# Block-causal attention feeding a top-1 mixture of experts: GpSimd split of the first expert's weights, its subtraction, and a new order of steps for two batches

## The chip, the cores and the metric

One core of one Trainium2 chip runs the whole program as a single launch. The metric is device time in microseconds (us); the time before is the median of three runs. The engines are TensorE (PE; its weight loads are PEld), VectorE (DVE), ScalarE (ACT), GpSimd (POOL) and the queue of SyncE (SP), which issues most DMAs.

## What is computed

Attention over 8 batches, 8 heads, 576 positions and head size 64, masked by blocks of 64, in float32. Its output, 4608 tokens of 512 numbers, goes through a top-1 mixture of 8 experts:

```python
logits = x @ w_gate
e_idx = argmax(logits)                       # one expert per token
gate_w = exp(logits - max)[e_idx] / (sum(exp(logits - max)) + 1e-9)
eom = 1 / (1 + exp(-(x @ w_output_gate)))
for e in range(8):
    mask = e_idx == e
    ye = relu(x[mask] @ w1[e]) @ w2[e]       # w1 512x1024, w2 1024x512
    out[mask] = gate_w[mask] * eom[mask, e] * ye
```

## The kernel before

**Attention.** The program walks 32 pairs of heads (p = 0 to 31, four to a batch b). Pair p's scores and softmax, pair p-1's transposes and pair p-2's products with V are interleaved by a table, `PLAN` (line 299). Its names are: S0 to S4, the scores of the five query tiles on PE; M0 to M4, their row maxima and the scaled biases on DVE (lines 396, 400, 404); E0 to E4, the exponentials on ACT (line 411; A and B are the two heads); F0 to F6, the transposes of the probabilities on PE (lines 445, 458); C0 to C6, the copies of these out of PSUM on ACT (line 1084); V0, V1 and VM, the products with V on PE (lines 480, 488); X and XM, the copies of these on ACT. Two PSUM buffers hold scores, so S2 of a pair needs E4 of the pair before it to have read its buffer, and S1 of a pair needs E3. On PE, DVE and ACT the program order is the written order. On GpSimd and SP a scheduler sets it. Each engine works its own queue strictly in order.

**Turns.** Each "|" of PLAN is a turn, eight to a pair (0 to 7): every running generator of the list `later` advances to its next `yield`. In PLAN turn 0 and turn 1 come after C0, turn 2 after E0B, turn 3 after C4, turn 4 after M3, turn 5 after VM, turn 6 after M4 and turn 7 right behind it, before XM.

**A batch's end.** `finish_batch` (line 497) plays the 32 steps of `finish_steps` (line 505) for a batch whose four pairs are done; `pace` is how many steps go into a turn: 1 for batches 0 to 4 (four pairs long), 2 for batches 5 and 6 (two pairs long), 3 for batch 7. The steps: `logits` (PE, line 538) and `keep` (ACT, line 544), `turn_logits` and `turn_last` (PE), `scale_logits` and `scale_last` (DVE, lines 567, 579); `heads` (lines 587, 588) adds the heads' shares, on GpSimd for batches 0 to 4 and on DVE for 5 to 7; `choose` (DVE, lines 591 to 599) finds the maximum `mx` and the chosen expert `oh`, with `z` on GpSimd (line 600); `ranks`, `own` and `slots` find each token's place; `turn` and `store`, T(t) and K(t), write the five tiles of x out; `excess` (DVE, line 629) is `d = lg - mx`, `shares` (ACT, line 632) its exponential, `gather` three small sums on DVE (lines 635 to 637), `gate` an exponential on ACT (line 640), `weights` the token's weight on DVE (lines 643, 644), and `scatter` five indirect DMAs on GpSimd into the routing table (line 650).

**The first expert.** `load_first` (line 902) starts in pair 28. It picks the expert with most tokens of batches 0 to 5, fetches the ids (line 834) and rows (line 845) of its first tokens behind batch 5's scatter, and loads w1 and then w2 in four chunks of 128x1024. The chunks of w2 reuse the buffers of w1's. Each chunk is split into a high half (float16) and a low half (bfloat16): on GpSimd, `split` (line 872) does a chunk in four quarters of 128x256, each a cast (line 878) and a subtraction (line 879). The experts' matmuls (lines 1001 and 1030) begin after the attention; for all later experts the split is ACT's cast and DVE's subtraction (lines 874, 875).

Of the kernel before, what the change touches and what calls it, by code (L numbers as in the profile page):

```python
# [1 line left out]

# [7 lines left out]
BF16 = mybir.dt.bfloat16  # L10
# [4 lines left out]
ALU = mybir.AluOpType  # L15
# [11 lines left out]
def block_attention_top1_moe(  # L27
# [11 lines left out]
    nc = tc.nc  # L39
# [456 lines left out]

    def finish_batch(b, sums, xT, pace):

        for i, fns in enumerate(finish_steps(b, sums, xT)):
            for fn in fns:  # L500
                fn()
            if i % pace == pace - 1:
                yield

    def finish_steps(b, sums, xT):

        rec = small.tile([P, NT, H], F32, name="rec")
        lgT = sb.tile([P, S], F32, name="lgT", bufs=1)
# [10 lines left out]
        se = small.tile([P, NT], F32, name="se")  # L519
        sli = small.tile([P, NT], I32, name="sli")  # L520
        held = {}

        def bank():
            return ps_t.tile([P, 512], F32, name="ps_t")
# [18 lines left out]
        def keep(c0, c1):  # L543
            nc.scalar.copy(lgT[:, c0:c1], held[c0][:, 0:c1 - c0])  # L544

        def turn(t):
            r = ROWS[t]
            held["r", t] = pm = bank()
            for g in range(NP):
                nc.tensor.transpose(pm[0:r, P * g:P * g + P], xT[:, g, Q0[t]:Q0[t] + r], ident)  # L550

        def store(t):
            r = ROWS[t]
            xn = sb.tile([P, DM], F32, name="xn", bufs=4)
            nc.vector.tensor_tensor(
                xn[0:r].rearrange("p (h d) -> p h d", d=D), held["r", t][0:r].rearrange("p (h d) -> p h d", d=D),
                rec[0:r, t].unsqueeze(2).broadcast_to([r, H, D]), ALU.mult,
            )
            nc.sync.dma_start(x_d[b * S + Q0[t]:b * S + Q0[t] + r, :], xn[0:r])
# [22 lines left out]
            )  # L582

        def heads():
            eng = nc.gpsimd if b < B - 3 else nc.vector
            for w in (4, 2):
                eng.tensor_tensor(lh[:, :, 0:w], lh[:, :, 0:w], lh[:, :, w:2 * w], ALU.add)
            eng.tensor_tensor(L, lh[:, :, 0], lh[:, :, 1], ALU.add)

        def choose():  # L590
            nc.vector.tensor_reduce(mx, lg, AX.X, ALU.max)
            eq = small.tile([P, NT, E], F32, name="eq")
            nc.vector.tensor_tensor(eq, lg, mxb, ALU.is_equal)
            nc.vector.tensor_tensor(eq, eq, erev.unsqueeze(1).broadcast_to([P, NT, E]), ALU.mult)
            nc.vector.tensor_reduce(er, eq, AX.X, ALU.max)
            nc.vector.tensor_tensor(
                oh, er.unsqueeze(2).broadcast_to([P, NT, E]), erev.unsqueeze(1).broadcast_to([P, NT, E]), ALU.is_equal
            )
            nc.vector.memset(oh[64:128, LAST, :], 0.0)
            nc.gpsimd.tensor_tensor(z, lz, oh, ALU.mult)  # L600

        def ranks():
            held["p"] = pr = ps_a.tile([P, 512], F32, name="ps_a")
# [14 lines left out]
        def slots():  # L618
# [5 lines left out]
            sl = small.tile([P, NT], F32, name="sl")  # L624
            nc.vector.scalar_tensor_tensor(sl, er, -float(NTOK), rank, ALU.mult, ALU.add)
            nc.vector.tensor_scalar(sli, sl, float(E * NTOK), None, ALU.add)

        def excess():
            nc.vector.tensor_tensor(d, lg, mxb, ALU.subtract)

        def shares():
            nc.scalar.activation(d, d, AF.Exp)
# [13 lines left out]
        def scatter():  # L646
# [13 lines left out]

        big, end = (0, 512), (512, S)
        T, K = (lambda t: lambda: turn(t)), (lambda t: lambda: store(t))
        steps = [
            [lambda: logits(*end)], [lambda: keep(*end), lambda: logits(*big)], [lambda: keep(*big), recips], [turn_logits],
            [scale_logits], [turn_last], [scale_last], [heads],
            [], [], [T(0)], [K(0)], [], [choose], [], [],
            [], [T(1), ranks], [own, K(1), T(2)], [K(2)], [T(3), slots], [K(3)], [], [],
            [excess], [shares], [T(4)], [K(4)], [], [gather], [gate], [weights, scatter],
        ]
        return steps if b < B - 1 else [fns for fns in steps if fns]  # L670

# [198 lines left out]
                        tc.add_manual_dep(chained[0].ins, after.name, SYNC, reason="after the ids")  # L870

    def split(eng, hi, lo, src):
        if eng is nc.vector:
            nc.scalar.copy(hi, src)  # L874
            eng.tensor_tensor(lo, src, hi, ALU.subtract)  # L875
            return
        for at in quarters(src):
            eng.tensor_copy(hi[at], src[at])
            eng.tensor_tensor(lo[at], src[at], hi[at], ALU.subtract)

    def quarters(src):
        _, g, n = src.shape
# [19 lines left out]
    def load_first():  # L902

        route_first()
        fetch_ids(steps[0])
        fetch_ids(steps[1], (0, 1))
        fetch_x(steps[0])
        fetch_x(steps[1], (0, 1))
        with chain():
            ev = nc.sync.value_load(f_i[0:1, 0:1], min_val=0, max_val=E - 1)  # L910

        wc = {}

        def load(w, c):
            dt, nm = ((F16, "hh"), (BF16, "hl"))[c % 2]
            wc[c] = fs.tile([P, KF, 2, P], dt, name=nm).rearrange("p f h n -> p (f h n)").bitcast(F32)
            nc.sync.dma_start(quarter(w, wc[c]), rows_of(w, ev, c))

        for c in range(4):
            load(w1, c)  # L920
        for w, fn, r0, r1 in ((w1, split_w1, 13, 3), (w2, split_w2, 2, 2)):
            for r in range(r0):
                yield
            for c in range(4):
                fn(nc.gpsimd, 0, wc[c], c)
                if w is w1:
                    load(w2, c)
                for r in range(r1):
                    yield

    def buf(i):
        return 0 if i < 2 else (i - 1) % 2
# [337 lines left out]
```

## Time and profile before

| what | value |
|---|---|
| runs, us | 819.75 median (811.24, 819.75, 820.64) |
| the profiled execution | 814.11 us, of which the span is 812.4 us |
| PE busy | 734.6 us, 90% of the span |
| DVE, ACT, POOL busy | 546.8 (67%), 531.7 (65%), 339.4 us (42%) |
| attention and routing | about 0 to 440 us of the span; the experts from there to the end |

A row of a timeline is: start us, duration us, engine, line, operation, out<-in with shapes, how many instructions the row holds, and in brackets the idle time of that engine just before it and what ended it. L12 is line 12 of the kernel.

### The profile page before, as it was taken

What the parts mean: (1) busy time and instruction counts of PE and PEld (TensorE: products, weight loads), DVE (VectorE), ACT (ScalarE), POOL (GpSimd) and SP (SyncE); (2) the same over time, 40 slices, a digit from 0 to 9 for tenths busy, and PEclk for the clock granted to TensorE, in tenths of its full rate; (3) what the DMA queues carried; (4) which work ended last, traced back from release to release, by engine and by line L of the source; (5) the groups of instructions that cost most, each with busy time, mean ns of one, the idle gap of its engine ahead of it and who ended that gap; (6) DMA issues with size and microseconds to landing.
All of it is one profiled execution on the core that took longest, in us unless ns stands there. A gap on an engine that the chain in (4) does not pass through costs nothing. (4 is left out here: it accounts for less than half of the span.)

```text
span 812.4 us, 18753 instructions
## 1 busy us (share of the span) xinstructions
PE 734.6 (90%) x6918; PEld 516.4 (64%) x6918; DVE 546.8 (67%) x1060; ACT 531.7 (65%) x1189; POOL 339.4 (42%) x495
## 2 busy tenths in 40 slices
PE   5799999899999988843999999999999999999994
PEld 3577767666676656523676666956668566686652
DVE  6566867767676858588573786957679666795530
ACT  4799879788888876712511777855578655785530
POOL 5667755564747421494224732322422232410001
PEclk9899999999999999975999999999999999999998
DMA  8899988968884645641116799799999979731601
GB/s 157 163 187 198 222 180 149 226 139 185 148 204 90 138 83 134 162 128 28 47 60 231 186 274 297 230 282 332 315 303 364 297 156 332 239 73 40 234 28 42
DMA packets 256630, 147.88 MB, mean 182 GB/s; under 512 B 224144, under 2 KB 224208, under 8 KB 256528
## 3 DMA queue, kind: packets, MB, share of 16 engines
q1 hardware_dynamic: 248416, 127.30, 62.9%
q0 software_dynamic: 8112, 19.29, 7.6%
q8 instruction: 56, 0.92, 0.5%
q14 instruction: 46, 0.38, 0.2%
HBM read 126.03 MB, written 19.34 MB: 179 GB/s over the span
## 5 line engine op out<-in xcount | busy, mean ns | idle before, releaser
L1001 PEld LDWEIGHTS <-w1b 128*128 128x128 f16 (+1 forms) x2208 | 176.6, 98 | 25.3 <-issue 3.9
L411 ACT ACTIVATE pt<-ps_s,nbs 128x512 f32<-128x512 f32 (+4 forms) x282 | 155.2, 572 | 37.6 <-DVE nbs L404 35.9
L1001 PE MATMUL ps_s<-xt,w1b 128*128 128x256 f16 (+5 forms) x1920 | 175.5, 253 | 0.9 <-issue 0.4
L1030 PE MATMUL ps_t<-w2b,hh 128*128 128x512 f16 (+1 forms) x560 | 166.5, 379 | 0.0
L875 DVE TENSOR_TENSOR w2b<-w2f,w2b 128x1024 bf16<-128x1024 f32 x80 | 92.7, 1219 | 90.6 <-ACT w2b L874 77.7
L396 DVE TENSOR_REDUCE nmx<-ps_s 128x2 f32<-128x1024 f32 (+1 forms) x125 | 102.7, 821 | 64.2 <-PE ps_s L381 40.9
L1084 ACT COPY pT<-ps_t 128x512 f32<-128x512 f32 (+1 forms) x221 | 112.1, 555 | 36.2 <-PE ps_t L445 28.1
L1039 POOL DMA_INDIRECT out_dram<-ys,ids x38 | 51.8, 1363 | 161.0 <-ACT ys L1038 91.2
L445 PE MATMUL ps_t<-ident,pt 128*128 128x128 f32 x768 | 112.4, 283 | 5.5 <-ACT pT L1084 2.1
L1030 PE MATMUL ps_t<-w2b,hl 128*128 128x512 f16 x280 | 106.1, 379 | 0.0
L1038 ACT ACTIVATE ys<-ps_t,ids 128x512 f32<-128x512 f32 (+1 forms) x38 | 26.1, 686 | 111.8 <-PE ps_t L1030 95.5
L445 PEld LDWEIGHTS ps_t<-ident,pt 128*128 128x128 f32 x768 | 87.2, 144 | 15.8 <-ACT lgT L544 4.2
L1030 PEld LDWEIGHTS <-hh 128*128 128x128 f16 x560 | 54.3, 98 | 61.7 <-issue 0.7
L875 DVE TENSOR_TENSOR w1b<-w1f,w1b 128x1024 bf16<-128x1024 f32 x80 | 92.7, 1217 | 0.8 <-ACT w1b L874 0.7
L103 POOL TENSOR_TENSOR sp<-nat,sp 128x320 f16<-128x320 f32 x120 | 86.7, 742 | 3.9 <-DVE sp L102 2.5
L379 PE MATMUL ps_s<-tr,tr 128*128 128x512 f16 (+1 forms) x250 | 73.3, 309 | 12.6 <-ACT pt L411 12.5
L874 ACT CAST w1b<-w1f 128x1024 f16<-128x1024 f32 x80 | 78.4, 1045 | 2.8 <-DMA w1f<-in_moe_w_dram 2.4
L874 ACT CAST w2b<-w2f 128x1024 f16<-128x1024 f32 x80 | 77.7, 1043 | 0.4 <-DVE w2b L875 0.2
L480 PE MATMUL ps_a<-pT,va 128*64 128x384 f32 (+2 forms) x256 | 74.0, 412 | 0.0
L480 PE MATMUL ps_a<-pT,vb 128*64 128x384 f32 (+2 forms) x256 | 74.0, 412 | 0.0
L650 POOL DMA_INDIRECT tab_d<-idg,sli x40 | 38.9, 973 | 83.7 <-DVE idg L644 54.2
L380 PE MATMUL ps_s<-sw,tr 128*128 128x512 f16 (+1 forms) x250 | 71.3, 307 | 2.4 <-DVE sw L201 2.4
(220 smaller groups left out, 1206.5 us busy)
## 6 DMA issues: line engine op xcount, KB each, us to landing
w1f<-in_moe_w_dram SPq DMA_DIRECT2D x80, 512.0 KB
w2f<-in_moe_w_dram SPq DMA_DIRECT2D x80, 512.0 KB
nat<-in_k_dram SPq DMA_DIRECT2D x15, 576.0 KB
nat<-in_q_dram SPq DMA_DIRECT2D x15, 576.0 KB
x_d<-xn SPq DMA_DIRECT2D x32, 256.0 KB
va<-in_v_dram SPq DMA_DIRECT2D x32, 128.0 KB
vb<-in_v_dram SPq DMA_DIRECT2D x32, 128.0 KB
hh<-in_moe_w_dram SPq DMA_DIRECT2D x4, 512.0 KB
```

Source lines behind the costliest of these rows:

```text
L103: last_lo[0] = lo.tensor_tensor(sp[:, sl, 1, :], self.nats[i][:, sl], sp[:, sl, 0, :], ALU.subtract)
L379: nc.tensor.matmul(o, qq, k1[ab][:, 0:n], start=True, stop=False)
L380: nc.tensor.matmul(o, qq, k2[ab][:, 0:n], start=False, stop=False)
L396: nc.vector.tensor_reduce(nmx[t], at[t], AX.X, ALU.max, negate=True)
L411: last_exp[0] = nc.scalar.activation(probs[t][:, ab * n:(ab + 1) * n], at[t, ab], AF.Exp, bias=nbs[t][:, ab:ab + 1], scale=SCALE, accum_ou ...
L445: nc.tensor.transpose(held[i][:, P * j:P * j + P], probs[t][:, sl], ident)
L480: nc.tensor.matmul(pa[half, c0:512], vs[a][:, j, :], rows[:, a, j, c0 - P:512 - P], start=(j == 0), stop=(j == 3))
L874: nc.scalar.copy(hi, src)
L875: eng.tensor_tensor(lo, src, hi, ALU.subtract)
L1001: nc.tensor.matmul(ph[:, f4].rearrange("p (h n) -> p h n", n=w), wv[:, cc, f, :], xv[:, cc], start=(k == 0), stop=(k == 3 * KD - 1))
L1030: nc.tensor.matmul(py, hv[:, f, h], wv[:, f, :], start=(k == 0), stop=(k == 3 * KF - 1))
L1084: (nc.vector.tensor_copy if p >= B * NP and name in ("C1", "C3", "C5", "X") else nc.scalar.copy)(to, of)
```

## The change

The split of w1 moves to a generator of its own, `split_slowly`, that issues one quarter (cast and subtraction) per turn, sixteen in all. The split of w2 on GpSimd keeps only the subtractions; its casts, one of 128x1024 per chunk, go to ACT, a chunk per turn. `excess` is gone as a step: `d` is computed inside `choose`, on GpSimd for batches 0 to 5 and on DVE for 6 and 7; `z` and `heads` follow the same rule, so `heads` of batch 5 goes to GpSimd. Batches 5 and 6 get a list of steps of their own, one entry per turn. In the list of the others `shares` moves from turn 25 to 21, K(3) from 21 to 22, and `gather`, `gate`, `weights` and `scatter` each one turn earlier.

```diff
+        eng = nc.gpsimd if b < B - 2 else nc.vector
...
         def heads():
-            eng = nc.gpsimd if b < B - 3 else nc.vector
...
-            nc.gpsimd.tensor_tensor(z, lz, oh, ALU.mult)
+            eng.tensor_tensor(z, lz, oh, ALU.mult)
+            eng.tensor_tensor(d, lg, mxb, ALU.subtract)
...
+        lge, lgb, ke, kb = (partial(f, *c) for f in (logits, keep) for c in (end, big))
+        if pace == 2:
+            return [
+                [lge, lgb], [ke], [kb, recips], [turn_logits, turn_last], [scale_logits, T(0)], [scale_last, heads, K(0)], [], [choose],
+                [], [T(1), ranks], [own, K(1), T(2)], [K(2)], [slots, shares, T(3)], [gather, gate], [K(3), weights, scatter, T(4)], [K(4)],
+            ]
         steps = [
-            [lambda: logits(*end)], [lambda: keep(*end), lambda: logits(*big)], [lambda: keep(*big), recips], [turn_logits],
-            [scale_logits], [turn_last], [scale_last], [heads],
+            [lge], [ke, lgb], [kb, recips], [turn_logits], [scale_logits], [turn_last], [scale_last], [heads],
             [], [], [T(0)], [K(0)], [], [choose], [], [],
-            [], [T(1), ranks], [own, K(1), T(2)], [K(2)], [T(3), slots], [K(3)], [], [],
-            [excess], [shares], [T(4)], [K(4)], [], [gather], [gate], [weights, scatter],
+            [], [T(1), ranks], [own, K(1), T(2)], [K(2)], [T(3), slots], [shares], [K(3)], [],
+            [], [], [T(4)], [K(4)], [gather], [gate], [weights, scatter], [],
         ]
...
     def split(eng, hi, lo, src):
-        if eng is nc.vector:
-            nc.scalar.copy(hi, src)
-            eng.tensor_tensor(lo, src, hi, ALU.subtract)
-            return
+        nc.scalar.copy(hi, src)
+        for at in [(slice(None),) * 3] if eng is nc.vector else quarters(src):
+            eng.tensor_tensor(lo[at], src[at], hi[at], ALU.subtract)
+
+    def split_slowly(hi, lo, src):
         for at in quarters(src):
-            eng.tensor_copy(hi[at], src[at])
-            eng.tensor_tensor(lo[at], src[at], hi[at], ALU.subtract)
+            with tc.issue_after(last_exp[0].ins):
+                nc.gpsimd.tensor_copy(hi[at], src[at])
+                nc.gpsimd.tensor_tensor(lo[at], src[at], hi[at], ALU.subtract)
+            yield
...
+        for r in range(11):
+            yield
+        for c in range(4):
+            yield from split_slowly(w1b[0][:, 0, c], w1b[0][:, 1, c].bitcast(BF16), wc[c].rearrange("p (g m) -> p g m", g=KF))
+            load(w2, c)
+        for r in range(5):
+            yield
+        for c in range(4):
+            with tc.issue_after(last_exp[0].ins):
+                split_w2(nc.gpsimd, 0, wc[c], c)
+            yield
```

On DVE, in pair 30 (batch 6's end begins there), `heads` (line 587) stands ahead of M2 and M3 (`nmx_5723`, `nmx_5724`) before:

```order
L396 TENSOR_REDUCE nmx_5721<-ps_s 128x2
L404 TENSOR_SCALAR nbs_5726<-nmx_5721 128x1 x2
L567 TENSOR_TENSOR lh<-ps_t,rec 128x512
L579 TENSOR_TENSOR lh<-ps_t,rec 64x128
L587 TENSOR_TENSOR lh<-lh 128x5x64
L587 TENSOR_TENSOR lh<-lh 128x5x32
L588 TENSOR_TENSOR L<-lh 128x80
L396 TENSOR_REDUCE nmx_5723<-ps_s 128x2
L404 TENSOR_SCALAR nbs_5728<-nmx_5723 128x1 x2
L396 TENSOR_REDUCE nmx_5724<-ps_s 128x2
L404 TENSOR_SCALAR nbs_5729<-nmx_5724 128x1 x2
L555 TENSOR_TENSOR xn<-ps_t,rec 128x512
```

and after the change, on the same engine at the same place (`heads` is line 588, M2 and M3 are `nmx_5725` and `nmx_5726`, M4 is `nmx_5727`):

```order
L397 TENSOR_REDUCE nmx_5725<-ps_s 128x2
L405 TENSOR_SCALAR nbs_5730<-nmx_5725 128x1 x2
L397 TENSOR_REDUCE nmx_5726<-ps_s 128x2
L405 TENSOR_SCALAR nbs_5731<-nmx_5726 128x1 x2
L569 TENSOR_TENSOR lh<-ps_t,rec 128x512
L581 TENSOR_TENSOR lh<-ps_t,rec 64x128
L588 TENSOR_TENSOR lh<-lh 128x5x64
L588 TENSOR_TENSOR lh<-lh 128x5x32
L589 TENSOR_TENSOR L<-lh 128x80
L557 TENSOR_TENSOR xn<-ps_t,rec 128x512
L401 TENSOR_REDUCE nmx_5727<-ps_s 128x1
L405 TENSOR_SCALAR nbs_5732<-nmx_5727 128x1
```

M2 and M3 moved ahead of `scale_logits` and `heads`; behind `heads` now stand K(0) (line 557) and M4.

On GpSimd, the end of w1's split and the start of w2's, before (in brackets what an instruction waits for: a DMA queue, or an engine):

```order
L879 TENSOR_TENSOR w1b_5353<-hh,w1b_5353 128x256 [waits Pool_49] x2
L878 CAST w1b_5353<-hl 128x256 [waits DMAHW7_49]
L878 CAST w1b_5353<-hl 128x256
L879 TENSOR_TENSOR w1b_5353<-hl,w1b_5353 128x256 [waits Pool_49] x2
L878 CAST w1b_5353<-hl 128x256 x2
L879 TENSOR_TENSOR w1b_5353<-hl,w1b_5353 128x256 [waits Pool_49] x2
L878 CAST w2b_5354<-hh 128x256 [waits DMAHW2_49]
L878 CAST w2b_5354<-hh 128x256
L879 TENSOR_TENSOR w2b_5354<-hh,w2b_5354 128x256 [waits Pool_49] x2
```

and after (line 884 is the cast and 885 the subtraction of `split_slowly`, line 649 the scatter of batch 6, line 879 w2's subtractions):

```order
L885 TENSOR_TENSOR w1b_5353<-hh,w1b_5353 128x256 [waits Pool_49] x2
L884 CAST w1b_5353<-hl 128x256 [waits DMAHW5_49]
L884 CAST w1b_5353<-hl 128x256
L885 TENSOR_TENSOR w1b_5353<-hl,w1b_5353 128x256 [waits Pool_49] x2
L884 CAST w1b_5353<-hl 128x256 x2
L885 TENSOR_TENSOR w1b_5353<-hl,w1b_5353 128x256 [waits Pool_49] x2
L535 MEMSET lh 64x128 [waits DVE_49,Pool_49]
L649 DMA tab_d<-idg,sli 37120x2 [waits DVE_49]
L649 DMA tab_d<-idg,sli 37120x2 x4
L879 TENSOR_TENSOR w2b_5354<-hh,w2b_5354 128x256 [waits DMAHW1_49,Activation_49,Pool_49]
L879 TENSOR_TENSOR w2b_5354<-hh,w2b_5354 128x256 x3
L879 TENSOR_TENSOR w2b_5354<-hl,w2b_5354 128x256 [waits DMAHW5_49,Activation_49]
```

The quarters of w1 keep their order and their waits, for their DMA and for GpSimd itself; none waits for ACT. The subtractions of w2 moved behind the scatter of batch 6, and wait for ACT's casts.

On ACT, in the last pair of batch 4's end, `shares` (line 632) stands before E4 (128x576) before:

```order
L1084 COPY xT<-ps_a 128x512
L1084 COPY xT<-ps_t 128x64
L1084 COPY pT<-ps_t 128x2x2x128
L632 ACTIVATE d<-d 128x40
L411 ACTIVATE pt_4756,sums<-ps_s,nbs_4538 128x576
L1084 COPY pT<-ps_t 128x4x128 x2
```

and after the change (line 631) ahead of E3 of the pair before that:

```order
L1093 COPY pT<-ps_t 128x128
L631 ACTIVATE d<-d 128x40
L412 ACTIVATE pt_4704,sums<-ps_s,nbs_4538 128x512 x2
L1093 COPY xT<-ps_a 128x512
L1093 COPY xT<-ps_t 128x64
L1093 COPY pT<-ps_t 128x2x2x128
L412 ACTIVATE pt_4756,sums<-ps_s,nbs_4539 128x576
```

It moved ahead by E3's two exponentials and three copies. Further on in the same pair `gate` (line 640) stands behind E3 (128x512) and X before:

```order
L1084 COPY pT<-ps_t 128x128
L411 ACTIVATE pt_4885,sums<-ps_s,nbs_4725 128x512 x2
L1084 COPY xT<-ps_a 128x512
L640 ACTIVATE zs<-zs 128x5
L1084 COPY xT<-ps_t 128x64
L1084 COPY pT<-ps_t 128x2x2x128
```

and after the change (line 639) ahead of E3:

```order
L1093 COPY pT<-ps_t 128x128
L639 ACTIVATE zs<-zs 128x5
L412 ACTIVATE pt_4886,sums<-ps_s,nbs_4727 128x512 x2
L1093 COPY xT<-ps_a 128x512
L1093 COPY xT<-ps_t 128x64
```

E3's two exponentials are now queued behind `gate`. The four casts of w2 on ACT stand in pair 32 (transposes and products of pairs 31 and 30 only): behind XM, C0, C2 and C4 of that stretch, one each in turns 0 to 3, with E4 between the second and the third.

## Rows read from the trace of the kernel before

**Rows 1.** Stretches: length, busy us of PE, PEld, DVE, ACT, POOL; clock, DMA, GB/s.

```profile
340.00:360.00 20.00, 11.44 (x91) 7.58 (x91) 14.57 (x15) 6.33 (x19) 19.36 (x37) 0.89 0.43 131
360.00:380.00 20.00, 2.75 (x31) 2.23 (x31) 17.16 (x9) 3.82 (x12) 14.01 (x30) 0.50 0.14 37
```

**Rows 2.** Waits, all of the span: us in total, times, longest us.

```profile
ACT pt L411 <- DVE nbs L404: 37.5, 32, 25.6
```

**Rows 3.** Timeline of PE: S4 (L388) of eight pairs, S1 (L379), T0 (L550), ranks (L604).

```profile
157.63 0.39 PE L388 MATMUL ps_s<-tr,tr 128*64 128x512 f16 x2
...
170.55 0.39 PE L388 MATMUL ps_s<-tr,tr 128*64 128x512 f16 x2
...
289.45 0.39 PE L388 MATMUL ps_s<-tr,tr 128*64 128x512 f16 x2
...
291.15 0.27 PE L379 MATMUL ps_s<-tr,tr 128*128 128x256 f16 x1
...
302.91 0.41 PE L388 MATMUL ps_s<-tr,tr 128*64 128x512 f16 x2 [0.97 <-ACT pt L411]
...
304.13 0.66 PE L550 MATMUL ps_t<-ident,xT 128*128 128x128 f32 x4
...
307.58 0.18 PE L604 MATMUL ps_a<-oh,below 128*128 128x40 f16 x1 [1.11 <-DVE oh L599]
...
315.93 0.39 PE L388 MATMUL ps_s<-tr,tr 128*64 128x512 f16 x2
...
338.73 0.39 PE L388 MATMUL ps_s<-tr,tr 128*64 128x512 f16 x2
...
377.25 0.64 PE L388 MATMUL ps_s<-tr,tr 128*64 128x512 f16 x2 [23.50 <-ACT pt L411]
...
391.87 0.39 PE L388 MATMUL ps_s<-tr,tr 128*64 128x512 f16 x2
```

**Rows 4.** Timeline of DVE, pair 30: first step of batch 6's heads.

```profile
349.15 25.37 DVE L587 TENSOR_TENSOR lh<-lh 128x320 f32<-128x320 f32 x2
```

**Rows 5.** Timeline of GpSimd: first ids, then w1's and w2's split.

```profile
336.37 0.76 POOL L834 DMA_DIRECT2D ids<-tab_d  x1 [9.20 <-DMA tab_d<-idg,sli]
...
343.44 1.29 POOL L879 TENSOR_TENSOR w1b<-hh,w1b 128x256 bf16<-128x256 f32 x2
...
358.27 0.73 POOL L878 CAST w2b<-hh 128x256 f16<-128x256 f32 x2
...
372.53 1.28 POOL L879 TENSOR_TENSOR w2b<-hl,w2b 128x256 bf16<-128x256 f32 x2
```

**Rows 6.** A stretch after a short idle time of PE, columns as in rows 1.

```profile
346.00:348.00 2.00, 2.00 (x10) 1.44 (x9) 0.61 (x2) 1.35 (x3) 2.00 (x6) 0.50 0.08 20
```

**Rows 7.** Timeline of PE: S2 after batch 0's and batch 4's shares.

```profile
106.17 0.32 PE L379 MATMUL ps_s<-tr,tr 128*128 128x384 f16 x1 [1.29 <-ACT pt L411]
...
283.37 0.32 PE L379 MATMUL ps_s<-tr,tr 128*128 128x384 f16 x1 [1.29 <-ACT pt L411]
```

**Rows 8.** Timeline of ACT: batch 4's shares.

```profile
282.36 0.24 ACT L632 ACTIVATE d<-d 128x40 f32<-128x40 f32 x1 [1.28 <-DVE d L629]
```

**Rows 9.** Timeline of DVE: batch 4's gather, first and last of three.

```profile
290.00 0.20 DVE L635 TENSOR_REDUCE se<-d 128x5 f32<-128x40 f32 x1
...
290.31 0.19 DVE L637 TENSOR_REDUCE zs<-z 128x5 f32<-128x40 f32 x1
```

**Rows 10.** Timeline of ACT: end of an E3; two copies of pair 32.

```profile
290.40 0.20 ACT L411 ACTIVATION_READ_ACCUMULATOR pt<-ps_s,nbs 128x1 f32 x1
...
395.67 0.58 ACT L1084 COPY pT<-ps_t 128x512 f32<-128x512 f32 x1 [0.75 <-PE ps_t L445]
...
398.32 0.27 ACT L1084 COPY pT<-ps_t 128x128 f32<-128x128 f32 x1 [0.65 <-PE ps_t L458]
```

**Rows 11.** Timeline of DVE: batch 1's excess.

```profile
149.03 1.47 DVE L629 TENSOR_TENSOR d<-L,mx 128x40 f32<-128x40 f32 x1
```

**Rows 12.** Groups by cost: ACT's cast of a chunk of w2.

```profile
L874 ACT CAST w2b<-w2f 128x1024 f16<-128x1024 f32 x80 | 77.7, 1043 | 0.4 <-DVE w2b L875 0.2
```

More of the change, by code (lines that the diff above doesn't have):

```diff
@@ L1 @@
+from functools import partial
 from contextlib import ExitStack, contextmanager, nullcontext
@@ L497, in finish_batch, with finish_steps @@
     def finish_batch(b, sums, xT, pace):
-        for i, fns in enumerate(finish_steps(b, sums, xT)):
+        for i, fns in enumerate(finish_steps(b, sums, xT, pace)):
             for fn in fns:
                 fn()
-            if i % pace == pace - 1:
+            if pace < 3 or i % pace == pace - 1:
                 yield
-    def finish_steps(b, sums, xT):
+    def finish_steps(b, sums, xT, pace):
         rec = small.tile([P, NT, H], F32, name="rec")
@@ L626, in slots @@
             nc.vector.tensor_scalar(sli, sl, float(E * NTOK), None, ALU.add)
-        def excess():
-            nc.vector.tensor_tensor(d, lg, mxb, ALU.subtract)
         def shares():
@@ L920, in load_first @@
             load(w1, c)
[L921 to L929, printed above, removed]
+        for r in range(11):
[9 more added lines that the diff above has]
+            yield
     def buf(i):
```

## The prediction

> **What bounds the kernel now.** I read the page's slices first. PE is busy in nearly every slice but for a hole between 350 and 380 us, so PE sets the time almost everywhere, and what can be won lies where PE waits. The stretches put numbers on the hole: in the 20 us from 360 PE is busy 2.75 us, and its clock is granted at 0.50, the lower of its two levels, 1.2 GHz [rows 1]. The waits name it: ACT waited once for 25.6 us for DVE's `nbs`, the biased maxima [rows 2]. The timelines then give the chain. PE's S4 of pair 30 waited 23.50 us for ACT to free a score buffer, at 377.25 [rows 3]. ACT waited for M2, and M2 stood on DVE behind `heads` of batch 6, whose first addition began at 349.15 and held DVE for 25.37 us with its second [rows 4]. GpSimd was at that time splitting w1 and w2 without a gap, until 373.81 [rows 5]; DVE's addition ended right after it. So an addition whose two inputs lie in SBUF was kept out as long as GpSimd's queue ran on. That is the wait to follow.
>
> Two smaller things follow from the same views. PE's clock falls after shorter idle times too: at 346 to 348, where PE worked without a gap after a far shorter wait in the same pair, it was 0.50 [rows 6]. And PE lost 1.29 us at 106.17 and at 283.37, always at the same place [rows 7]; there are five such rows, one for each of batches 0 to 4, 1.29, 2.57, 1.29, 1.39 and 1.29 us, 7.83 in all. Before each of them ACT waited as long for DVE's `d` [rows 8]: `shares` stood on ACT ahead of E4, while `d` stood on DVE behind M1 of the next pair, and S2 needs E4's buffer.
>
> **Batches 0 to 4.** `d` is now made on GpSimd beside `z`, eight turns ahead of `shares`, so these five waits go: -7.83. What comes late next is `gate`. It now stands on ACT ahead of E3, and needs `gather`, which DVE begins when M3 is done and ends 0.50 us later (290.00 to 290.50) [rows 9]. With an exponential of 0.24 [rows 8], E3 starts 0.74 later. E3 ended at 290.60 [rows 10], S1, which needs its buffer, started at 291.15 [rows 3]: of 0.74, 0.55 was slack and 0.2 remains. I take 0.3 for each batch, 1.5 in all; the ends are 0 and 3.7. K(3) behind M4 and one operation less on DVE are hidden behind PE's transposes. Sum: -6.3.
>
> **Batch 5.** Pair 26 took 13.46 us from S4 to S4 (289.45 to 302.91), 0.97 of it a wait because `heads` stood ahead of M2 [rows 3]. The new list spreads logits as the longer list does, whose first pair took 12.92 (157.63 to 170.55); with T0's transposes of 0.66 moved into it this makes 13.5, no gain. Pair 27 took 13.02. It loses T0, 0.66, and about half of the 1.11 that PE waited for `oh` before the ranks [rows 3], since `heads` on GpSimd is slower but begins earlier: 11.9. Together 25.4 for 26.5: -1.1; the ends are +1 and -3.
>
> **Batch 6.** Pairs 30 and 31 took 53.1 (338.73 to 391.87) [rows 3]. By the same list they would take 25.4 with no wait on GpSimd. But the sixteen quarters of w1 are not paced on the chip: in the order GpSimd's queue after the change holds them back to back, and none waits for ACT. Before, the 32 quarters of w1 and w2 less the first two casts (0.73) took from 343.44 to 373.81 [rows 5]: 31.1 us with these casts, 0.97 a quarter, 15.5 for sixteen. They follow the first ids, which waited 9.20 us for the scatter of batch 5 [rows 5]. That scatter comes about 2 us earlier (weights one turn earlier, `gate` ahead of E3), so I put the quarters at 341 to 356.5 on the clock of the trace of before, where pair 30's counting begins at S4, 338.73. `heads` now stands behind M3, two us ahead of the next S4, which would be at 338.73 + 13.5 = 352.2: it is reached at 350.5. If GpSimd keeps DVE out as before, DVE waits 6 us, and behind `heads` stand K(0) and M4. M4 comes about 5.3 late; the products, transposes and scores between S4 and the next S2 cover about 1.2 of it, so PE stands 4 us. M2, M3, and with them E2 and E3, are no longer behind it. After 4 us the clock will have fallen, as in rows 6: at half speed for some 4 us another 2. Taken: 6. The ends are 0, if DVE is let in, and 9, if the quarters run two us later and the clock takes longer. So 25.4 + 6 = 31.4 for 53.1: -21.7.
>
> Here the Trainium skill speaks against this reading. SBUF — State Buffer, "SBUF: two separate sides", says that VectorE and GpSimd share a port pair as an exclusive lock: whichever instruction starts first has it for that whole instruction, and the other blocks. The trace agrees that `heads` was blocked [rows 4], but it was blocked over some 50 instructions of GpSimd, not one. By the page DVE would wait for one of them, and the sum would be that of the first rival below.
>
> The trace has a row for the milder case as well: batch 1's `excess`, an operation on 40 columns, took 1.47 at 149.03 beside GpSimd's splits of q and k, and was let in while these went on [rows 11]. I take the row nearest to the case: the same addition against the same split.
>
> **The casts and subtractions of w2.** Four casts of 1.04 go to ACT [rows 12], in pair 32, one ahead of each of C0, E4, C4 and C6. ACT idled there 0.75 and 0.65, waiting for transposes [rows 10]; of 4.2 us this covers 1.4, and PE, which needs the copies for its products, waits for the rest: +2.8. The ends are 0 and 4.2. The sixteen subtractions, 0.65 each, run on GpSimd behind the scatter of batch 6, 10.4 us; only `heads` of batch 7 on DVE can meet them, more than a pair later: +0.5, the ends 0 and 4. The expert's first product with w2 comes later still.
>
> **The sum.** -6.3 - 1.1 - 21.7 + 2.8 + 0.5 = -25.8. The profiled execution took 814.1, so 788.3. It lay 5.6 below the median of the three runs (819.75); a run's place among them is chance, and I add half of that: **791**. Two per cent of the median, about what a measurement of this kernel can tell, is 16.4 us: 803.4 is the border.
>
> **The rivals.**
> *DVE is let in at the next instruction of GpSimd.* Then `heads` of batch 6 waits 0.66, PE does not stand there, and the 6 us go: 785. For it: rows 11. Against it: rows 4. It would also be the result if the quarters were paced after all; the order shows no wait for it. The page named above, SBUF — State Buffer of the Trainium skill, would have it so.
> *The new lists cost what they save.* ACT gets `gate` ahead of E3 and the casts ahead of the copies; if no slack is left, that is 2.2 more for the gates, 1.4 for the casts, 1.5 more in each of the four pairs 26, 27, 30 and 31 (as S4 of pair 27 lost 0.97 to such a wait), and 3 where batch 7's `heads` meets w2's subtractions: 791 + 13 = 804, within two per cent.
> *Slower: ACT waits for w2 itself.* The first cast of w2 on ACT stands ahead of C0, and a chunk of w2 is loaded only when its buffer is free, after w1's chunk is split. If a load lands late, ACT, and behind it PE, wait one us for each us. It decides from some 29 us late: 820 and more. Before, GpSimd split w1's first chunk by about 347 and cast w2's first at 358.27 with no idle time ahead [rows 5], so such a load took 11 us at most. Now the first buffer is free at about 345, and ACT comes to its first cast near 372 (two us after 338.73 + 31.4): the load would have to take over 50.
>
> **How the numbers follow.** The forecast gets 0.57, its own range 783 to 800 (its ends: gates 3.7 for 1.5, stall 3 either way, casts 4.2). The first rival gets 0.26, the second 0.14, the third 0.03. Faster by over 2%: nearly all of the first two and about four in ten of the second rival, 0.88; within 2%: 0.10; slower 0.02. The range goes from 776, the first rival with no cost of the gates and the casts half hidden, to 804, the second.
>
> **What would show it.** Right: no ACT wait for `d` before E4 in batches 0 to 4, and no idle time of PE over 1 us at S2 there; one long DVE addition in `heads` of batch 6, 5 to 8 us, that ends with the last subtraction of w1; PE idle some 4 us at the S2 after it; S4 to S4 of about 13.5 and 12 in pairs 26 and 27; four casts ahead of copies in pair 32 with PE waiting for ACT. Wrong: `heads` of batch 6 under 2 us (first rival), GpSimd's quarters with gaps of a turn between them, or a new PE wait over 5 us anywhere between 290 and 440 us.

## The result, and the profile after

| what | before | after |
|---|---|---|
| median of the runs, us | 819.77 (4 runs, 811.24 to 820.64) | 792.94 (4 runs, 791.08 to 795.41) |
| ratio, with its 95% interval | | 0.970 (0.963 to 0.977): faster |
| the profiled execution, of which the span | 814.11, 812.4 | 794.42, 792.8 |

The forecast was 791. I read the profile after in the order of the prediction. First the two stretches of [rows 1]:

```profile
340.00:360.00 20.00, 8.81 (x60) 5.87 (x58) 18.21 (x21) 7.79 (x25) 12.98 (x27) 0.70 0.46 134
360.00:380.00 20.00, 18.89 (x198) 13.74 (x196) 12.98 (x46) 15.07 (x40) 3.97 (x4) 0.96 0.25 76
...
352.00:356.00 4.00, 0.00 (x0) 0.00 (x0) 3.74 (x11) 1.23 (x4) 0.78 (x2) 0.50 0.72 188
...
358.00:360.00 2.00, 2.00 (x10) 0.86 (x10) 0.69 (x1) 1.95 (x6) 0.20 (x1) 0.50 0.00 0
```

From 360 on PE is busy again (18.89 us where it was 2.75). A hole is left between 340 and 360, with the clock at 0.50 as in [rows 6]. The waits of PE from 30 to 290 us, where the five rows of [rows 7] stood (us in total, times, the longest), have nothing over 0.8 us left for S2 (line 380):

```profile
PE ps_s L380 <- ACT pt L412: 2.1, 5, 0.8
```

The timeline of PE after the change, S4 (now line 389) of pairs 17, 18, 25 to 27 and 29 to 31, with what stands between (a pair is counted from the S4 before it to its own, so pair 18 runs from 198.36 to 213.59):

```profile
198.36 0.39 PE L389 MATMUL ps_s<-tr,tr 128*64 128x512 f16 x2
...
202.44 1.09 PE L446 MATMUL ps_t<-ident,pt 128*128 128x128 f32 x8
...
204.87 0.65 PE L446 MATMUL ps_t<-ident,pt 128*128 128x128 f32 x4 [0.62 <-ACT pT L1093]
206.97 0.66 PE L446 MATMUL ps_t<-ident,pt 128*128 128x128 f32 x4 [1.45 <-issue]
213.59 0.39 PE L389 MATMUL ps_s<-tr,tr 128*64 128x512 f16 x2
...
288.50 0.39 PE L389 MATMUL ps_s<-tr,tr 128*64 128x512 f16 x2
302.83 0.39 PE L389 MATMUL ps_s<-tr,tr 128*64 128x512 f16 x2
313.87 0.39 PE L389 MATMUL ps_s<-tr,tr 128*64 128x512 f16 x2
...
336.38 0.39 PE L389 MATMUL ps_s<-tr,tr 128*64 128x512 f16 x2
356.70 1.12 PE L446 MATMUL ps_t<-ident,pt 128*128 128x128 f32 x4 [11.19 <-DVE lh L569]
361.21 0.56 PE L389 MATMUL ps_s<-tr,tr 128*64 128x512 f16 x2
371.95 0.39 PE L389 MATMUL ps_s<-tr,tr 128*64 128x512 f16 x2
374.89 2.53 PE L446 MATMUL ps_t<-ident,pt 128*128 128x128 f32 x20 [1.10 <-ACT xT L1093]
381.21 0.27 PE L489 MATMUL ps_t<-pT,va 128*64 128x64 f32 x1 [0.63 <-DVE pT L1093]
```

PE stood 11.19 us in pair 30 for `scale_logits` (line 569), whose bank the transposes need. Pairs 30 and 31 took 35.57 us (336.38 to 371.95), 53.14 before [rows 3]. What stood ahead of `scale_logits` on DVE, after the change:

```profile
340.51 0.21 DVE L405 TENSOR_SCALAR nbs<-nmx 128x1 f32<-128x1 f32 x2
340.64 12.19 DVE L529 TENSOR_SCALAR sums<-sums 128x36 f32<-128x36 f32 x1
352.86 0.35 DVE L530 RECIPROCAL rec<-sums 128x32 f32<-128x32 f32 x1
...
356.87 0.85 DVE L588 TENSOR_TENSOR lh<-lh 128x320 f32<-128x320 f32 x2
```

The first operation of `recips` held DVE for 12.19 us; `heads`, the one that took 25.37 before [rows 4], took 0.85 for its two. The small `nbs`, from SBUF to SBUF as well, took 0.21 for two ahead of it, with GpSimd already splitting w1. GpSimd after the change, the first ids, then the first and the last rows of w1's split:

```profile
328.10 0.76 POOL L838 DMA_DIRECT2D ids<-tab_d  x1 [4.59 <-DMA tab_d<-idg,sli]
...
337.20 0.75 POOL L884 CAST w1b<-hh 128x256 f16<-128x256 f32 x2
337.91 1.30 POOL L885 TENSOR_TENSOR w1b<-hh,w1b 128x256 bf16<-128x256 f32 x2
...
351.50 1.28 POOL L885 TENSOR_TENSOR w1b<-hl,w1b 128x256 bf16<-128x256 f32 x2
```

The sixteen quarters ran back to back from 337.20 to 352.78, 15.6 us, and DVE's operation ended 0.05 behind them. Each row begins before the one ahead of it has ended (337.20 + 0.75 is 337.95, the next begins at 337.91), so the rows show no pause in the run.

And ACT, `gate` of batch 6 and the first and last cast of w2:

```profile
372.71 0.21 ACT L639 ACTIVATE zs<-zs 128x5 f32<-128x5 f32 x1 [1.67 <-DVE zs L636]
...
374.71 1.07 ACT L877 CAST w2b<-hh 128x1024 f16<-128x1024 f32 x1
...
379.70 1.10 ACT L877 CAST w2b<-hl 128x1024 f16<-128x1024 f32 x1
```

By stretches of the span, the prediction's terms and what the two profiles show:

| stretch | predicted | measured | from |
|---|---|---|---|
| to S4 of pair 25 | -6.3 | -0.95 | 289.45 to 288.50 |
| pairs 26, 27 | -1.1 | -1.1 | 26.48 to 25.37 |
| pairs 28, 29 | 0 | -0.3 | 22.80 to 22.51 |
| pairs 30, 31 | -21.7 | -17.6 | 53.14 to 35.57 |
| from there to the end | +3.3 | +0.3 | 420.5 to 420.9 |
| sum | -25.8 | -19.6 | 812.4 to 792.8 |

### The profile page after: what moved, and what is told of

The parts are those of the page before. It is cut to its first block, busy times and chain, and to the rows that moved or that the text cites. A ratio compares the mean times of both kernels' runs of the same rounds, so it can differ in the third digit from the quotient of the medians.

```text
span 792.8 us, 18737 instructions
## 1 busy us (share of the span) xinstructions
PE 733.3 (92%) x6918; PEld 514.5 (65%) x6918; DVE 532.0 (67%) x1053; ACT 535.3 (68%) x1193; POOL 341.9 (43%) x486
## 5 line engine op out<-in xcount | busy, mean ns | idle before, releaser
L412 ACT ACTIVATE pt<-ps_s,nbs 128x512 f32<-128x512 f32 (+4 forms) x282 | 155.2, 572 | 18.2 <-DVE nbs L405 17.1
L446 PE MATMUL ps_t<-ident,pt 128*128 128x128 f32 x768 | 112.2, 282 | 24.2 <-DVE lh L569 12.1
L1048 POOL DMA_INDIRECT out_dram<-ys,ids x38 | 47.0, 1236 | 153.2 <-ACT ys L1047 72.9
L446 PEld LDWEIGHTS ps_t<-ident,pt 128*128 128x128 f32 x768 | 85.8, 143 | 37.5 <-DVE lh L569 12.5
L481 PE MATMUL ps_a<-pT,va 128*64 128x384 f32 (+2 forms) x256 | 76.5, 423 | 0.0
L481 PE MATMUL ps_a<-pT,vb 128*64 128x384 f32 (+2 forms) x256 | 76.5, 423 | 0.0
```

Of the source, the lines that this page charges most:

```text
L412: last_exp[0] = nc.scalar.activation(probs[t][:, ab * n:(ab + 1) * n], at[t, ab], AF.Exp, bias=nbs[t][:, ab:ab + 1], scale=SCALE, accum_ou ...
L446: nc.tensor.transpose(held[i][:, P * j:P * j + P], probs[t][:, sl], ident)
L481: nc.tensor.matmul(pa[half, c0:512], vs[a][:, j, :], rows[:, a, j, c0 - P:512 - P], start=(j == 0), stop=(j == 3))
```

## The experiments

Twelve runs, in four groups. The groups ran on different chips: the kernel before had medians of 806.0 (e1 to e4), 819.2 (e5 to e8), 803.3 (e9 to e11) and 818.1 us (e12). Each ratio is against the kernel before on the same chip.

### One part of the change at a time (e1, e2, e7)

e1, the turns of batches 0 to 4 with `d` on GpSimd, in the kernel before:

```diff
+            if b < B - 3:
+                nc.gpsimd.tensor_tensor(d, lg, mxb, ALU.subtract)
...
+        if b < B - 3:
+            steps = steps[:20] + [
+                [T(3), slots], [shares], [K(3)], [],
+                [], [], [T(4)], [K(4)], [gather], [gate], [weights, scatter], [],
+            ]
```

> The kernel before, with the part of the change for batches 0 to 4 alone: d on GpSimd in choose, shares, K(3), gather, gate, weights and scatter at their new turns. By the prediction's first term the five waits of PE at S2 (7.83 us) go and the gates cost 1.5: 6.3 us less than before, about 813.5. The rival, read from the trace after the change: the waits go, but PE then loses about as much in the transposes of the first pair of batches 2 to 4 (pairs of 15.2 and 15.7 us where there were 12.8); then 1 us less than before, about 818.8, and the same long first pairs are seen here.

Measured: 797.69, ratio 0.990 (0.987 to 0.994), 8.3 us less by the medians. e2, the new `split`, `split_slowly` and `load_first` in the kernel before:

```diff
-        for w, fn, r0, r1 in ((w1, split_w1, 13, 3), (w2, split_w2, 2, 2)):
...
+            yield from split_slowly(w1b[0][:, 0, c], w1b[0][:, 1, c].bitcast(BF16), wc[c].rearrange("p (g m) -> p g m", g=KF))
...
+                split_w2(nc.gpsimd, 0, wc[c], c)
```

> The kernel before, with the new split alone (w1 in sixteen quarters by split_slowly, w2 cast on ACT), the lists of steps as they were. By the theory that GpSimd's unbroken run keeps DVE out, the run is half as long: it ends about 357 us, and heads of batch 6, begun at about 349, is held 8 to 9 us where it was 25.4. So 17 us less than before, about 803. The rival, that the stall needs the new order of steps to shrink: no change, 817 to 820. If the casts on ACT cost the 2.8 us predicted, PE waits for ACT's copies in the pair after the last one.

Measured: 792.05, ratio 0.983 (0.979 to 0.986), 14 us less. The timelines of PE, S4 (line 388) of pairs 1 and 25, in e1:

```profile
32.27 0.41 PE L388 MATMUL ps_s<-tr,tr 128*64 128x512 f16 x2 [0.44 <-ACT pt L411]
...
277.41 0.39 PE L388 MATMUL ps_s<-tr,tr 128*64 128x512 f16 x2
```

and in e2, which has batches 0 to 4 as before, with S4 of pair 30:

```profile
32.72 0.41 PE L388 MATMUL ps_s<-tr,tr 128*64 128x512 f16 x2 [0.31 <-ACT pt L411]
...
285.86 0.39 PE L388 MATMUL ps_s<-tr,tr 128*64 128x512 f16 x2
...
354.51 0.64 PE L388 MATMUL ps_s<-tr,tr 128*64 128x512 f16 x2 [10.89 <-ACT pt L411]
```

From pair 1 to 25 e1 takes 245.14 us and e2 253.14: the new turns give 8.0 on this chip, all of the five waits and nothing for the gates. In e2 the first addition of DVE's `heads` was held 12.41 us (8 to 9 were expected), where the two together had taken 25.37 [rows 4], and PE stood 10.89 where it was 23.50 [rows 3]:

```profile
339.02 12.41 DVE L587 TENSOR_TENSOR lh<-lh 128x320 f32<-128x320 f32 x1
```

From S4 of pair 31 to the end e1, with the old split, takes 417.5 and e2, with the casts on ACT, 419.1: the casts cost 1.5 at most. e7, the new list with its `heads`, `z` and `d`, in the kernel before:

```diff
+        if pace == 2:
+            return [
+                [lge, lgb], [ke], [kb, recips], [turn_logits, turn_last], [scale_logits, T(0)], [scale_last, heads, K(0)], [], [choose],
...
```

> The kernel before with the new list of steps for batches 5 and 6 alone (with its heads, z and d on GpSimd for batch 5). By the theory that the length of GpSimd's run sets the stall, an operation of batch 6's end on DVE is still held until the last subtraction of w2, some 23 us or more, pairs 30 and 31 take 48 us or more, and the time falls by 1 to 2. The rival, that moving M2 and M3 ahead of heads is what removed the wait: pairs 30 and 31 take 31 to 36, and the time falls by 15 or more.

Measured: 812.64, ratio 0.991 (0.988 to 0.994), 6.6 us less. `recips` was held from 344.48 until the last subtraction of w2:

```profile
344.48 28.75 DVE L527 TENSOR_SCALAR sums<-sums 128x36 f32<-128x36 f32 x1
```

So the list alone doesn't take the stall away (pairs 30 and 31 took 53.2), but it gave more than the 1 to 2 expected. Against the trace of before on the same chip (e6, 7.6 us longer) 2.4 lie in pairs 30 and 31 and 3.2 behind S4 of pair 31; where these come from is not shown. It is the half as long run of GpSimd that halves the stall (e2). The three parts alone gave 8.3, 14 and 6.6 us, on two chips, and the whole change 26.8 and, in e5, 25.3.

### The two kernels again, on one chip (e5, e6)

No edit: the changed kernel, and the kernel before for a trace.

> The changed kernel as it is, for a trace on the same chip as the runs beside it. If the long first pairs of batches 3 and 4 (15.2 and 15.7 us) come from the change, they are here too, and the S4 of pair 25 comes about 1 us earlier than in the kernel before on this chip. If they come from the execution or the chip, these pairs take about 11 us here, and the S4 of pair 25 comes 6 to 8 us earlier. In pairs 30 and 31 some operation of DVE on SBUF alone in recips or heads of batch 6 is held until the last subtraction of w1, and PE stands 6 to 11 us: the time is 10 us over that of the paced version.

> The kernel before as it is, for a trace on this chip. heads of batch 6 is held about 25 us, until the last subtraction of w2. The five waits of PE at S2 (1.3 to 2.6 us) are there; whether the first pairs of batches 2 to 4 take 12.8 us, as in the first trace, or 10.7, shows what of that is the execution's.

Measured: e5 793.87, ratio 0.970 (0.966 to 0.974); e6 one run of 821.95. In both it is `recips` that is held, 12.46 us in e5 and 28.60 in e6, from there to the end of GpSimd's run. That differs from e6's own expectation: in the profile of before `heads` was held and `recips` was not. In e1, e2 and e4 `recips` came ahead of the run, and `heads` was held. But in the profile of before `recips` came inside the run, 0.74 us behind its start [rows 5], as in e6, and was let in. The profile of before, then e6:

```profile
344.18 0.60 DVE L527 TENSOR_SCALAR sums<-sums 128x36 f32<-128x36 f32 x1
```

```profile
344.56 28.60 DVE L527 TENSOR_SCALAR sums<-sums 128x36 f32<-128x36 f32 x1
```

So the order of arrival alone does not decide which one is held, and no run shows what does. On this chip the long first pairs are there in e5 (16.0 us for pair 18, 17.1 for pair 22) and not in e6 (12.9 and 13.5), and S4 of pair 25 is as late as in e6 (289.63 and 289.13).

### What keeps DVE out (e4, e3, e10, e11)

e4 leaves one operation of `recips` out, in batch 6:

```diff
-            nc.vector.tensor_scalar(sums, sums, 1e-9, None, ALU.add)
+            if b != B - 2:
+                nc.vector.tensor_scalar(sums, sums, 1e-9, None, ALU.add)
```

> The changed kernel without the first operation of recips in batch 6 (the addition of 1e-9 to sums that are at least 1, which float32 does not show). If any operation of DVE on SBUF alone is kept out by GpSimd's run, the reciprocal behind it takes the 12 us, and the time stays at 793. If only certain forms are, the reciprocals go through in under 1 us, M2 and M3 are not late, and the next that waits is heads, until GpSimd is through with w1 at about 353: PE stands some 4 us for 11.2, about 786 to 789.

Measured: 776.45, ratio 0.964 (0.959 to 0.968). On this chip GpSimd's first cast came at 327.38, when the reciprocals had begun (326.85), so the run says nothing on forms of operations. (The profile of before does: with GpSimd's run going on, the reciprocal at 344.82 took 0.35 us, its usual time, and the biases `nbs` took theirs in every trace.) It shows the prediction's own case: M2 and M3 go, and `heads` is held until the end of the run, with PE behind it; pairs 30 and 31 took 34.06 us, 9.4 over e3 on the same chip. DVE, then PE:

```profile
333.43 9.90 DVE L589 TENSOR_TENSOR lh<-lh 128x320 f32<-128x320 f32 x1
```

```profile
344.62 1.12 PE L553 MATMUL ps_t<-ident,xT 128*128 128x128 f32 x4 [6.36 <-DVE xn L558]
```

e3 paces the quarters in the way that the name of `split_slowly` says:

```diff
-                nc.gpsimd.tensor_copy(hi[at], src[at])
+                cast = nc.gpsimd.tensor_copy(hi[at], src[at])
+                tc.add_manual_dep(cast.ins, last_exp[0].ins.name, SYNC, reason="paced by the exponentials")
```

> The changed kernel, with each cast of w1's split on GpSimd made to wait for the exponential that was last written before it. By the theory that only an unbroken run of GpSimd keeps DVE out, the gaps let it in: the first operation of recips in batch 6 takes under 2 us for 12.19, pair 30 takes about 14 us from S4 to S4 for 24.83, and the time falls by 10 to 782. The rival, that the stall there comes with the new order of steps and not with GpSimd: pair 30 stays above 22 us and the time at 791 to 795. A third outcome: DVE is let in, but w1 is split later, w2 comes later, and ACT waits for it in pair 32: 784 to 790.

Measured: 770.56, ratio 0.957 (0.954 to 0.961). Pairs 30 and 31 took 24.67 (13.04 and 11.63), so nothing of the stall is the list's. `recips` began at 325.36, ahead of the first cast (325.47), and `heads` took 2.26:

```profile
331.95 2.26 DVE L588 TENSOR_TENSOR lh<-lh 128x320 f32<-128x320 f32 x2
```

It was let in although GpSimd's rows show no pause from 326.58 to 336.70. So e3 shows what the stall costs, not what ends it. e9 repeats it on another chip:

> The paced version once more, beside the two below on one chip. The ratio to before stays at about 0.957 if the gain does not hang on the chip. Where the kernel before takes about 819 us, the first pairs of batches 2 to 4 (pairs 14, 18 and 22) take 14 us or more as in the changed kernel, since pacing doesn't touch them: the ratio is then 0.957 to 0.960 (10 us less than the changed kernel's 0.970).

Measured: 769.81, ratio 0.958 (0.954 to 0.961). `heads` took 1.51 us for its two, again with no pause in GpSimd's rows. The third run of the same order, e10, was meant for another question:

```diff
-            [], [], [T(4)], [K(4)], [gather], [gate], [weights, scatter], [],
+            [], [], [T(4)], [K(4)], [gather], [gate], [weights], [],
+            *[[]] * 6, [scatter], [],
```

> The paced version, with the scatters of batches 0 to 4 eight turns later, in the pair after. If the scatter is what makes ACT and PE stand in the first pair, the stall moves with it: pairs 14, 18 and 22 fall to about 10.8 us, pairs 15, 19 and 23 rise from 9.6 to 11 to 14, and the time is the same within 3 us. If it is the logits beside the scatter that do it, the first pairs fall and nothing rises: 2 to 5 us less for each of batches 2 to 4, 6 to 15 us in all, where the chip shows the stall. If neither, the first pairs stay as long as in the paced version.

Measured: 769.68, ratio 0.958 (0.955 to 0.961). The question stays unanswered, as the scheduler put the scatters back where they were: GpSimd's order is that of e9, row for row. As a repeat it shows that pacing by ACT is not reliable. Here `heads` was held 4.76 us for its two additions, until GpSimd's run stopped by itself at 335.80, at an instruction that waits for `heads`. DVE, then GpSimd:

```profile
331.75 4.76 DVE L588 TENSOR_TENSOR lh<-lh 128x320 f32<-128x320 f32 x2
```

```profile
334.50 1.30 POOL L887 TENSOR_TENSOR w1b<-hh,w1b 128x256 bf16<-128x256 f32 x2
336.91 0.20 POOL L535 MEMSET lh<- 64x128 f32 x1 [1.10 <-DVE L L589]
```

e11 takes the pacing out and only puts GpSimd's instructions in the order in which they are written:

```diff
-            with tc.issue_after(last_exp[0].ins):
+            with tc.issue_after(last_exp[0].ins), tc.issue_after(last_sub[0].ins) if last_sub[0] else nullcontext():
                 nc.gpsimd.tensor_copy(hi[at], src[at])
-                nc.gpsimd.tensor_tensor(lo[at], src[at], hi[at], ALU.subtract)
+                last_sub[0] = nc.gpsimd.tensor_tensor(lo[at], src[at], hi[at], ALU.subtract)
```

> The changed kernel, not paced, with each cast of w1's split put behind the subtraction before it, so that GpSimd runs cast, subtraction, cast, subtraction, and each subtraction follows the cast it needs. No wait for ACT is added. If a short pause between two of GpSimd's instructions is enough to let DVE in (0.09 us in the paced version's trace, where a subtraction follows its own cast), no operation of recips or heads of batch 6 takes over 3 us, pair 30 takes about 13.5 us, and the time is that of the paced version within 2 us. If only a wait for another engine lets it in, 9 to 12 us of DVE's time are lost as in the changed kernel, and the time is 8 to 11 us over the paced version.

Measured: 767.77, ratio 0.955 (0.952 to 0.958). GpSimd's first rows of w1, then DVE's `recips` and `heads`:

```profile
325.53 0.41 POOL L884 CAST w1b<-hh 128x256 f16<-128x256 f32 x1
326.02 0.67 POOL L885 TENSOR_TENSOR w1b<-hh,w1b 128x256 bf16<-128x256 f32 x1
326.65 0.39 POOL L884 CAST w1b<-hh 128x256 f16<-128x256 f32 x1
327.11 0.67 POOL L885 TENSOR_TENSOR w1b<-hh,w1b 128x256 bf16<-128x256 f32 x1
```

```profile
325.75 0.23 DVE L529 TENSOR_SCALAR sums<-sums 128x36 f32<-128x36 f32 x1
...
332.33 1.20 DVE L588 TENSOR_TENSOR lh<-lh 128x320 f32<-128x320 f32 x2
```

Each subtraction now waits for the cast right ahead of it, and starts 0.08 us behind its end (325.94 to 326.02, 327.03 to 327.11; the rounded rows give 0.07 for the second). The sixteen quarters still fill 17.8 us of GpSimd, a little more than the 15.6 of the changed kernel, but a pause so short in each lets DVE in: no operation is held for a run any more.

### The casts of w2 (e8)

e8 is e3 with w2's casts on GpSimd again, each waiting for an exponential.

```diff
     def split(eng, hi, lo, src):
-        nc.scalar.copy(hi, src)
+        if eng is nc.vector:
+            nc.scalar.copy(hi, src)
         for at in [(slice(None),) * 3] if eng is nc.vector else quarters(src):
+            if eng is nc.gpsimd:
+                cast = eng.tensor_copy(hi[at], src[at])
+                tc.add_manual_dep(cast.ins, last_exp[0].ins.name, SYNC, reason="paced by the exponentials")
             eng.tensor_tensor(lo[at], src[at], hi[at], ALU.subtract)
```

> The paced version, with the casts of w2 on GpSimd again, each waiting for an exponential as w1's do. If ACT's four casts cost PE time, this is faster than the paced version by up to 2.8 us (the prediction's term), by about 1.5 if that was double what they cost. The rival: the casts on GpSimd keep DVE out in pair 32 or come ahead of the scatter of batch 6, and the time is the same or 2 to 5 us longer.

Measured: 789.54, ratio 0.964 (0.961 to 0.967), against 0.957 for e3 on another chip. The rival came: `heads` of batch 7 was held 5.72 us. DVE, then GpSimd:

```profile
381.53 5.72 DVE L588 TENSOR_TENSOR lh<-lh 128x320 f32<-128x320 f32 x2
```

```profile
385.81 0.39 POOL L881 CAST w2b<-hl 128x256 f16<-128x256 f32 x1
386.27 0.80 POOL L883 TENSOR_TENSOR w2b<-hl,w2b 128x256 bf16<-128x256 f32 x1
```

The last two rows show the mechanism once more. The cast ended at 386.19, its own subtraction began 0.08 later and took 0.80 for 0.66: there DVE came in, and both ran. From S4 of pair 31 to the end e8 takes 425.1 us, and e5, on the same chip with the casts on ACT, 422.0. Moving w2's casts back shows no gain, so they are better left on ACT.

### In order, on another chip (e12)

e12 joins e11's edit and e10's move of the scatters, without the pacing.

> The two together: w1's split in order (cast, subtraction, cast, subtraction), and the scatters of batches 0 to 4 eight turns later. Pairs 30 and 31 take about 24.2 us (13.04 and 11.15 in the run in order) with no operation of recips or heads of batch 6 over 3 us. Where the kernel before takes about 803 us, the first pairs are 10.8 to 11.1 with either place of the scatter, and the ratio is 0.955, as in order alone. Where it takes about 819 us: if the scatter makes ACT and PE stand, pairs 14, 18 and 22 fall from 14 to 17 us to about 10.8 and the pairs behind them rise, ratio 0.955 to 0.960; if the logits beside it are needed for the stall, nothing rises, and the ratio is 0.940 to 0.950; if the scatter has no part in it, the first pairs stay at 14 or more.

Measured: 779.66, ratio 0.953 (0.950 to 0.957); before 818.1 on this chip. The scatters stood where they were, as in e10, so it is e11 on a chip like that of the prediction. Pairs 30 and 31 took 25.34. `recips`, inside GpSimd's run (it began at 333.56), and `heads`:

```profile
336.01 0.20 DVE L529 TENSOR_SCALAR sums<-sums 128x36 f32<-128x36 f32 x1
...
342.76 1.20 DVE L588 TENSOR_TENSOR lh<-lh 128x320 f32<-128x320 f32 x2
```

On two chips the order cast, subtraction, cast, subtraction is faster than the kernel before by 4.5 and 4.7%; the change as made is by 3.0%, in both of its groups of runs. No chip ran both; on chips whose kernel before took 818 to 820 pairs 30 and 31 took 35.57 and 35.53 as changed (after, e5) and 25.34 in order (e12).

### What is left of batches 0 to 4

The first pairs of batches' ends (10, 14, 18 and 22) added up, S4 to S4:

| chip, by the median of before | steps as before | steps as changed |
|---|---|---|
| 818 to 820 | 51.5 (before), 52.2 (e6), 51.3 (e7) | 56.3 (after), 60.4 (e5), 60.1 (e8), 53.3 (e12) |
| 803 to 806 | 42.9 (e2) | 43.5 (e1), 43.7 (e3), 44.0 (e4), 43.5 (e9, e10 and e11) |

So some chips lose 2 us in each such pair whatever the steps, and with the new steps more, and less evenly. The rows of ACT after the change, pair 18, where PE waits at 204.87 and 206.97:

```profile
204.23 0.58 ACT L1093 COPY pT<-ps_t 128x512 f32<-128x512 f32 x1 [1.51 <-PE ps_t L446]
206.33 0.58 ACT L1093 COPY pT<-ps_t 128x512 f32<-128x512 f32 x1 [1.52 <-PE ps_t L446]
```

and of e11, the same copies in the same pair (S4 at 192.25; 4.78 behind it, where the first above is 5.87 behind):

```profile
197.03 1.08 ACT L1093 COPY pT<-ps_t 128x512 f32<-128x512 f32 x2 [0.44 <-PE ps_t L446]
```

The copies wait for the eight transposes that by the records ended at 203.53 (202.44 + 1.09), 0.7 and 2.8 us earlier, and PE then waits for the copies. What makes that wait, and why the new steps lengthen it, isn't settled: e10 and e12 were to move the scatter that runs at the same time, and didn't.

## Why the prediction came out right, and where its steps did not

**Batches 0 to 4: the term failed.** "-7.83 waits + 1.5 for the gates" gave -6.3; the chip of the prediction gave -0.95. The five waits did go: the fourth pairs (9, 13, 17, 21 and 25) took 47.6 us for 56.0, 8.4 less, with nothing for the gates. But the first pairs of batches' ends took 4.8 more (56.3 for 51.5) and the second pairs (11, 15, 19 and 23) 2.7 more (41.1 for 38.4). The step that failed is the sum that stops at the gates: PE's other waits were taken as fixed. Why the first pairs grew stays open. On a chip without the long first pairs the term was right and a little small (-8.0 in e1).

**Batch 5: right in its sum**, 25.37 us for 25.4; the parts were 14.33 and 11.04 where I had 13.5 and 11.9.

**Batch 6: the mechanism right, the operation wrong, the stall too small.** The quarters ran unpaced and back to back for 15.6 us (predicted 15.5), DVE was held to the end of them, and the rest followed. But I wrote that "`heads` of batch 6" is the one held, for 6 us, because `heads` was the one in the trace of before. `recips` stands three turns ahead of it, and works on SBUF alone too; in that trace it had been let in after 0.60 (344.18), beside the same run. After the change it came at 340.64, with the run 3.4 us old. The run began 0.8 us behind S4 of pair 29 (336.38), not 2.3 (341 against 338.73), as the first ids waited 4.59 us and not 9.20 [rows 5]. So M2 and M3, which I had as free, were late with it, and PE stood 11.19 us, not 4. By e3, where the same list without the stall takes 24.67, the stall's whole price is 10.9 (35.57 less 24.67), and by e12, on a chip like that of the prediction, 10.2 (35.57 less 25.34), not 6; the pairs without it were put at 25.4. Even the case that I had described, `heads` held and M2 and M3 free, cost 9.4 in e4, where it was held 9.90 for the 6 that I had put. Two of the signs that I had named for being wrong are there: `heads` of batch 6 took 0.85, and PE has a new wait of over 5 us. They do not speak for the first rival, as it was `recips` that was held; they say that the path to PE was another than mine. The clock behaved as in rows 6: 0.50 from 352 to 360.

**The casts: mis-sized.** "+2.8" and "+0.5" measured +0.3 in the two profiles, and at most 1.5 between e2 and e1; between e5 and e6 the same stretch, from S4 of pair 31 to the end, is 2.2 shorter with the casts on ACT (422.0 for 424.2). No cost stands clear of that spread. ACT's four casts stood at 374.71 to 380.80; the one PE wait of that stretch that a cast could have made is 0.63 (381.21). The 1.10 at 374.89 is behind `gate` of batch 6, for which ACT waited 1.67: this gate is not free as those of batches 0 to 4 were.

**The sum.** The terms missed by 6.1 us in the profiled runs (788.3 forecast, 794.42 measured): batches 0 to 4 gave 5.4 less than forecast and batch 6 4.1 less, and the casts took 3.0 less. The median still fell near 791, as the run profiled before lay 5.6 below its median and the one after 1.5 above: I had added half of the 5.6. So the total is right partly by luck.

**The rivals.** That DVE is let in at GpSimd's next instruction fell: 12.19 us beside some 25 instructions (12.5 quarters of 0.97). The rule of the Trainium skill (SBUF — State Buffer, "SBUF: two separate sides"), that the block lasts for one instruction, does not agree with that row, nor with 28.75 in e7; it agrees with e11, where a pause follows each cast and `heads` takes 1.20, and with the 0.60 of `recips` in the profile of before, which ended 0.05 behind one subtraction. That the lists cost what they save fell with e7 (6.6 us less) and e3 for batches 5 and 6; for batches 0 to 4 on the prediction's chip it came out nearly so (-0.95), though not at the gates. That ACT waits for w2 fell: the first cast, at 374.71, waited for nothing.

## What to carry to other kernels

A run of GpSimd without pauses can keep one DVE operation on SBUF out for the whole run, so look at every such operation behind the run's start and at what queues behind it, not only at the one that was hit last time. Before moving work away, try the order of GpSimd's own instructions: each one behind the one it needs leaves a pause of 0.08 us, and that was worth 10 to 11 us in pairs 30 and 31 (35.6 to 25.3 and 24.2), 1.2 to 1.4% of this kernel. Pacing by name or by the order of issue paces nothing where a scheduler sets the queue; read the queue's order and its waits.

## What the runs showed of the hardware that I had not expected

The block ends at a pause of 0.08 us between two instructions of GpSimd (e8, e11, e12), and in eight traces it held as long as each started before the one ahead had ended: 9.9 to 12.5 us beside sixteen quarters (after, e2, e4, e5), 25.0 to 28.8 beside thirty-two (before, e1, e6, e7). It is not a rule: with no pause that the rows show, the first addition of `heads` was through after 1.5 us in e3 and 0.80 in e9, and `recips` after 0.56 in e9 and 0.60 in the profile of before. What lets DVE in there is open. An operation with one input is held like one with two (12.19 for 0.17), but not each: `nbs` and the reciprocals took their usual times beside such a run. And chips differ by 16 us on the same kernel before (803.3 and 819.2), some 9 us of it in the first pairs of four batches' ends (51.5 to 52.2, and 42.9 in e2, whose steps there are those of before).
